# Where two operands of a matmul lie: the x tiles moved in front of the weights, 448 bytes apart modulo 512

## The chip, the cores and the metric

The kernel runs on one core of a Trainium2 chip. The metric is the device time of one execution in microseconds (us), given as the median of several runs. The engines are called PE (matmul), PEld (its weight loads), DVE, ACT, POOL and SP, as the profile calls them. Here SP issues the DMAs.

## What is computed

The reference has two stages. The first is a state space layer over 4 batches of 8 heads, 768 tokens, head width 32 and state width 16. For each chunk of tokens

```
y_intra = (C B^T * exp(cum_i - cum_j) * causal) @ x
y_inter = (C @ state) * exp(cum)
state   = exp(sum(log a)) * state + sum_j(B_j x_j^T * exp(cum_end - cum_j))
```

The second is a feed-forward layer over the resulting 3072 tokens of width 256:

```
h = x @ w_in          # 256 -> 2048
g = h - tanh(h)
out = g @ w_out       # 2048 -> 256
```

All inputs and the output are float32. The weights arrive as float64 bits.

## The kernel before

**State space layer.** A batch is cut into chunks of 112 tokens, 7 to a batch, the last of them 96 wide: 28 chunks. The first 16 rows of a chunk's operand hold the state that the chunk before left, so that one product of a chunk gives y_intra and y_inter at once. In `chunk_a`, PE makes the decay and the C B^T products (`att`, L459 and L465), ACT the exponential, DVE the product, POOL the causal cut, all in `lt`. In `chunk_y`, PE multiplies `lt` with `x` (L502, eight matmuls, one for each head) and then makes the state products, `x` with the weighted B in `bw` (L510, eight small matmuls). ACT copies the state to the next chunk's `x` (`fn_c`, L515), and ACT and DVE split y in two parts (`fn_h`, `fn_l`): `xh`, which holds y rounded to the type of the fast matmul (fp32r), and `xl`, the rest. The last chunk of a batch has no successor, and its state products are left out: `if not last:`.

**Feed-forward layer.** The weights are turned from float64 bits to the same two parts, `wh` and `wl`, which stay in the on-chip memory for the whole run (`conv`). A *step* is one slice of 128 of the 2048 hidden features for a tile of 512 tokens (256 in the first, narrow tiles). `mm1` (L553) is the first product: for each half k of the 256 inputs the matmuls `wh x xh` and `wl x xh`, and then `wh x xl` for both halves, six matmuls of 128 x 128 weights by 512 streamed columns, summed in one result buffer `ph`. ACT and DVE make g from `ph` and split it in `gh` and `gl`. `mm2` (L611) is the second product of a step: `wh x gh`, `wl x gh` and `wh x gl`, each for both halves of the 256 outputs, in the buffers `o` and `oe`: six matmuls again. PE loads the weights of the next matmul (PEld) while the current one streams.

**Order.** The class `Order` records every operation with its engine, a cost in microseconds and what it reads and writes. A list scheduler with random trials under a fixed seed (`plan`) sets the order in which they are issued on every engine. Its costs are constants of the code: the costs of `chunk_y` on PE are 0.5 for the last chunk of a batch and 0.7 for the others.

**Memory.** Tiles are placed one after the other in the order in which they are made. The tiles of the pool `cp` come first, `wh`, `wl`, `xh`, `xl` at its head; those of the other pools, `gh` and `gl` among them, lie behind. The addresses of the built programs, in bytes within a partition, and what is left of them modulo 512:

| tile | bytes | before: at | mod 512 | after: at | mod 512 |
|---|---|---|---|---|---|
| wh | 32768 | 16512 | 128 | 41152 | 192 |
| wl | 32768 | 49280 | 128 | 73920 | 192 |
| xh | 12288 | 82048 | 128 | 16512 | 128 |
| xl | 12288 | 94336 | 128 | 28800 | 128 |
| gh (first of 3) | 2048 | 216256 | 192 | 216704 | 128 |
| gl (first of 3) | 2048 | 222400 | 192 | 222848 | 128 |

A matmul of 512 columns streams 2048 bytes of `xh`, `xl`, `gh` or `gl` from a multiple of 512 behind the tile's start (1024 in the x tiles), and its weights are 512 bytes of `wh` or `wl`, again from a multiple of 512. So the distance of the streamed operand from the weights, modulo 512, is the same for all matmuls of a product: 0 in `mm1` and 64 in `mm2` before.

Of the kernel before, what the change touches and what calls it, by code (L numbers as in the profile page):

```python
# [10 lines left out]
F32 = mybir.dt.float32  # L11
F32R = mybir.dt.float32r
# [8 lines left out]
P = 128  # L21
NB, H, S, D, N = 4, 8, 768, 32, 16
# [7 lines left out]
NCK = NB * CPB  # L30
# [13 lines left out]
NPH, NL, NSW, NRAW, NGB, LAG, WARM = 2, 3, 4, 2, 3, 2, 8  # L44
SWEEPS = 0, 2, 4, 6, 8
NARROW = 1


class Order:
# [12 lines left out]
    def slot(self, tag, bufs):  # L62
        k = self.count[tag] = self.count.get(tag, -1) + 1
        self.fresh[f"{tag}#{k}"] = tag, f"{tag}#{k - bufs}"
        return f"{tag}#{k}"
# [144 lines left out]
def tile_ssm_moe(ctx: ExitStack, tc: tile.TileContext, a, x, bn, bc, wts, out):  # L210
    nc = tc.nc
    cp = ctx.enter_context(tc.tile_pool(name="cp", bufs=1))
# [73 lines left out]
            op("SP", 0.42, lambda i=i: fn(i), w=[name[i]], dma=4 * KB)  # L286


    wh = cp.tile([P, NCONV, 2, 2, 256], F32R, name="wh")
    wl = cp.tile([P, NCONV, 2, 2, 256], F32R, name="wl")  # L290
    xh = cp.tile([P, 2, 2 * S], F32R, name="xh")
    xl = cp.tile([P, 2, 2 * S], F32R, name="xl")

    def conv(u, halves=False):
        raw, n = raws[u, 0], 2 if halves else 1
# [68 lines left out]
    def qlen(ck):  # L364
        return QL if ck % CPB == CPB - 1 else Q
# [119 lines left out]
    def chunk_y(ck):  # L485

        d, k, q = grp[ck // CPG], chs[ck], qlen(ck)
        b, c = divmod(ck, CPB)
        cg = ck % CPG
        n_y = slot("y", 1) if ck in early else slot("ph", NPH)  # L490
        last = c == CPB - 1
        if c == 0:
            seq[b]["n_xh"] = op.pieces(slot("xh", 2), CPB)
            seq[b]["n_xl"] = op.pieces(slot("xl", 2), CPB)
        n_xh, n_xl = seq[b]["n_xh"][c], seq[b]["n_xl"][c]

        def fn():
            pool, tag = (ps_y, "y") if ck in early else (ps_h, "ph")
            y = k["y"] = pool.tile([P, 2 * H * D], F32, tag=tag, name=f"y{ck}")
            for hg in range(2):  # L500
                for h in range(4):
                    nc.tensor.matmul(out=y[D * h : D * h + D, hg * Q : hg * Q + q],  # L502
                                     lhsT=d["x"][:, cg, P * hg + D * h : P * hg + D * h + D],
                                     rhs=k["l"][:, 4 * hg + h, 0:q], start=True, stop=True)
            if not last:

                for w in range(2):
                    for i in range(4):
                        h = 2 * i + w
                        nc.tensor.matmul(out=y[D * i : D * i + N, H * D + D * w : H * D + D * w + D],  # L510
                                         lhsT=d["b"][:, cg, N * h : N * h + N], rhs=d["x"][:, cg, D * h : D * h + D],
                                         start=True, stop=True)

        def fn_c(i):
            nc.scalar.copy(grp[(ck + 1) // CPG]["x"][0:N, (ck + 1) % CPG, 2 * D * i : 2 * D * i + 2 * D],  # L515
                           k["y"][D * i : D * i + N, H * D : H * D + 2 * D])

        at = b % 2 * S + c * Q

        def fn_h():  # L520
            k["yv"] = k["y"][:, 0 : 2 * Q].rearrange("p (g q) -> p g q", g=2)[:, :, 0:q]
            nc.scalar.copy(xh[:, :, at : at + q], k["yv"])

        def fn_l():
            nc.vector.tensor_tensor(out=xl[:, :, at : at + q], in0=k["yv"],  # L525
                                    in1=xh[:, :, at : at + q].bitcast(F32), op=ALU.subtract)

        op("PE", 0.5 if last else 0.7, fn, r=[*k["n_l"], d["p_x"][cg], d["n_bw"]], w=[n_y])
        if not last:
            for i in range(4):  # L530
                op("ACT", 0.2, lambda i=i: fn_c(i), r=[n_y], w=[grp[(ck + 1) // CPG]["p_x"][(ck + 1) % CPG]])
        op("ACT", 0.36, fn_h, r=[n_y], w=[n_xh])
        op("DVE", 0.4, fn_l, r=[n_y, n_xh], w=[n_xl])
# [305 lines left out]
    for s, (i, j) in enumerate(zip(SWEEPS, SWEEPS[1:])):  # L839
        for w in narrow if s < NARROW else wide[: NSW * TT // TW]:  # L840
            segs.append((w, tuple(range(2 * i, 2 * j, TW // w[1]))))
# [84 lines left out]
```

## Time and profile before

| | |
|---|---|
| median of 3 runs | 348.45 us (347.52 to 348.57) |
| the profiled execution | 346.68 us |
| its span, first to last instruction | 345.0 us |
| mean granted TensorE clock | 0.98 |
| matmul records | 2700 (a float32 matmul has two, an fp32r or bf16 one has one) |
| PE busy, DVE busy, ACT busy | 95%, 66%, 56% of the span |

The busy share of PE comes from matmuls whose ends are modelled and which overlap, so it says that PE is not waiting, and not how fast it is. How fast it is shows in the distance of two starts in the timeline. Where the timeline joins two matmuls of one form in a row (x2), the row's start is that of the first.

### The profile page before, as it was taken

The page shows a single profiled execution, that of the slowest core. Times are in us where ns is not written, and L with a number is a line of the kernel's source. Part 1 is how long each engine was busy: PE and PEld are TensorE (multiplying, and loading weights), DVE is VectorE, ACT ScalarE, POOL GpSimd, SP SyncE. Part 2 cuts the span into 40 slices and gives each one's busy share as a digit, 9 for nine tenths or more (in the row PEclk, how much of TensorE's full clock was granted, in tenths as well). Part 3 has the DMA queues.
Part 4 walks back from the last instruction along what each step waited for, and adds up shares of the span by engine and source line. Part 5 has one row for each costly group of instructions (what it writes and reads, how often), then busy time and mean ns, then how long its engine had stood idle before and what let it go on. Part 6 is the DMA issues. An engine that isn't in the chain of part 4 may idle for free.

```text
span 345.0 us, 6725 instructions
## 1 busy us (share of the span) xinstructions
PE 326.9 (95%) x2700; PEld 264.6 (77%) x2700; DVE 229.4 (66%) x335; ACT 194.6 (56%) x399; POOL 55.4 (16%) x69
## 2 busy tenths in 40 slices
PE   7757889899999999999999999999999999999995
PEld 6647779787777878777777777777787777888883
DVE  5899989998889876654545656545655553644461
ACT  8876668786565535444555555545555553534441
POOL 1564534241001030000021111011110101000000
PEclk9978969999999999999999999999999999999999
DMA  6958593614101010111110131100010000010001
GB/s 172 299 163 233 133 260 88 217 34 137 42 0 30 1 46 10 51 63 44 28 36 0 31 91 30 30 2 2 0 63 2 2 0 0 2 61 0 2 0 61
DMA packets 10734, 21.25 MB, mean 62 GB/s; under 512 B 2656, under 2 KB 4384, under 8 KB 10704
## 3 DMA queue, kind: packets, MB, share of 16 engines
q1 hardware_dynamic: 10704, 20.84, 20.9%
q8 instruction: 21, 0.34, 0.4%
q14 instruction: 9, 0.07, 0.1%
HBM read 17.51 MB, written 3.32 MB: 60 GB/s over the span
## 4 chain that ended last, share of the span: by engine, by line
PE 86%; DVE 5%; DMA 4%; ACT 2%; issue 1%; SPq 1%; ACTq 0%
PE ph L553 39%; PE o L611 21%; PE oe L611 18%; PE y L502 4%; PE att L465 3%; DMA x<-x_d 2%; DMA raw<-w_d 2%; PE att L459 1%; DVE lt L473 1%; DVE g L573 1%; ACT x L515 1%; DVE wl L328 1%; PE y L510 1%; DVE rt_c L437 1%; DVE wm L317 1%
## 5 line engine op out<-in xcount | busy, mean ns | idle before, releaser
L569 ACT ACTIVATE g<-ph 128x512 f32<-128x512 f32 x96 | 57.5, 599 | 90.1 <-PE ph L553 82.9
L573 DVE TENSOR_TENSOR g<-ph,g 128x512 f32<-128x512 f32 x96 | 66.0, 690 | 61.0 <-ACT g L569 60.6
L583 DVE TENSOR_TENSOR gl<-g,gh 128x512 fp32r<-128x512 f32 x96 | 68.6, 720 | 27.4 <-ACT gh L577 26.3
L553 PE MATMUL ph<-xh,wh 128*128 128x512 f32 (+1 forms) x208 | 81.8, 395 | 0.4 <-DVE g L573 0.4
L553 PE MATMUL ph<-xh,wl 128*128 128x512 f32 (+1 forms) x208 | 79.5, 384 | 0.6 <-DVE wl L328 0.6
L577 ACT CAST gh<-g 128x512 fp32r<-128x512 f32 x96 | 59.2, 618 | 30.9 <-DVE g L573 25.4
L553 PE MATMUL ph<-xl,wh 128*128 128x512 f32 (+1 forms) x208 | 61.8, 379 | 0.0
L476 POOL TENSOR_SCALAR_AFFINE_SELECT lt<-lt 128x896 f32<-128x896 f32 (+1 forms) x25 | 31.7, 1267 | 163.0 <-DVE lt L473 163.0
L553 PEld LDWEIGHTS ph<-xh,wh 128*128 128x128 f32 x208 | 40.7, 196 | 8.8 <-DVE g L573 0.6
L553 PEld LDWEIGHTS ph<-xh,wl 128*128 128x128 f32 x208 | 40.6, 195 | 7.8 <-DVE wl L328 0.9
L553 PEld LDWEIGHTS ph<-xl,wh 128*128 128x128 f32 x208 | 39.1, 195 | 8.0
L611 PE MATMUL o<-gh,wh 128*128 128x512 f32 (+1 forms) x120 | 42.2, 384 | 0.0
L611 PE MATMUL o<-gh,wl 128*128 128x512 f32 (+1 forms) x120 | 39.6, 363 | 0.0
L611 PE MATMUL o<-gl,wh 128*128 128x512 f32 (+1 forms) x120 | 39.2, 359 | 0.0
L611 PE MATMUL oe<-gh,wh 128*128 128x512 f32 x88 | 34.7, 395 | 0.0
L611 PE MATMUL oe<-gh,wl 128*128 128x512 f32 x88 | 34.6, 394 | 0.0
L611 PE MATMUL oe<-gl,wh 128*128 128x512 f32 x88 | 34.6, 393 | 0.0
L473 DVE TENSOR_TENSOR lt<-att,lt 128x896 f32<-128x896 f32 (+1 forms) x25 | 26.6, 1065 | 4.0 <-ACT lt L469 3.8
L515 ACT COPY x<-y 16x64 f32<-16x64 f32 x96 | 19.5, 204 | 11.0 <-DVE xl L525 6.2
L611 PEld LDWEIGHTS o<-gh,wh 128*128 128x128 f32 x120 | 20.9, 188 | 5.2 <-DVE pt L632 0.4
L611 PEld LDWEIGHTS o<-gh,wl 128*128 128x128 f32 x120 | 20.9, 188 | 4.0
L469 ACT ACTIVATE lt<-att 128x896 f32<-128x896 f32 (+1 forms) x25 | 22.6, 903 | 2.3 <-PE att L465 1.4
(78 smaller groups left out, 326.4 us busy)
## 6 DMA issues: line engine op xcount, KB each, us to landing
raw<-w_d SPq DMA_DIRECT2D x16, 512.0 KB
x<-x_d SPq DMA_DIRECT2D x14, 256.0 KB
bc<-bc_d SPq DMA_DIRECT2D x56, 60.0 KB
out_d<-ob SPq DMA_DIRECT2D x12, 256.0 KB
braw<-bn_d SPq DMA_DIRECT2D x14, 112.0 KB
cum<-parts SPq DMA_DIRECT2D x1, 168.0 KB
lt_c<-cum SPq DMA_DIRECT2D x4, 27.0 KB
rt_c<-cum SPq DMA_DIRECT2D x4, 27.0 KB
```

The lines of the kernel that those rows point to most:

```text
L465: nc.tensor.matmul(out=at_[:, i, 2 + w, :], lhsT=bb[r, w], rhs=cc[r, w, 0:q], start=True, stop=True)
L469: nc.scalar.activation(k["l"][:, :, 0:q].rearrange("p (i w) q -> p i w q", i=4), k["a"][:, :, 0:2, :], AF.Exp)
L473: nc.vector.tensor_tensor(out=lt, in0=k["a"][:, :, 2:4, :], in1=lt, op=ALU.mult)
L476: nc.gpsimd.affine_select(out=k["l"][:, :, 0:q], in_=k["l"][:, :, 0:q], pattern=[[0, H], [1, q]], compare_op=ALU.is_ge, fill=0.0, base=N, ...
L502: nc.tensor.matmul(out=y[D * h : D * h + D, hg * Q : hg * Q + q], lhsT=d["x"][:, cg, P * hg + D * h : P * hg + D * h + D], rhs=k["l"][:, 4 ...
L515: nc.scalar.copy(grp[(ck + 1) // CPG]["x"][0:N, (ck + 1) % CPG, 2 * D * i : 2 * D * i + 2 * D], k["y"][D * i : D * i + N, H * D : H * D + ...
L553: nc.tensor.matmul(out=ph[:, j - f % 2, :], lhsT=w_[:, u, 0, k, j * P : (j + 1) * P], rhs=(xh, xl)[p][:, k, ts], start=p == 0 and k == 0 a ...
L569: nc.scalar.activation(g, gs[w, f][0], AF.Tanh)
L573: nc.vector.tensor_tensor(out=g, in0=ph, in1=g, op=ALU.subtract)
L577: nc.scalar.copy(gh, gs[w, f][1])
L583: nc.vector.tensor_tensor(out=gl, in0=g, in1=gh.bitcast(F32), op=ALU.subtract)
L611: nc.tensor.matmul(out=po[w, seg][e], lhsT=w_[:, u, 1, j, e * P : (e + 1) * P], rhs=g[:, j - f % 2, :], start=f == seg[0] and k == 0 and j ...
```

## The change

The change has two parts. The tiles `xh` and `xl` are made ahead of `wh` and `wl`. An unused tile of 64 bytes (`AHEAD` is 16 words) lies between them and the weights, and another of 384 bytes behind the weights. With that the distance of the streamed operand from the weights is 448 modulo 512 in both products (table above), and all tiles behind the weights stand 448 bytes higher. The other part: the last of the 28 chunks makes its state products too. They are written to a part of its result buffer that nobody reads. The costs that the scheduler sees stay as they were.

```
+AHEAD = 16
...
+    xh = cp.tile([P, 2, 2 * S], F32R, name="xh")
+    xl = cp.tile([P, 2, 2 * S], F32R, name="xl")
+    cp.tile([P, AHEAD], F32, name="ahead")
     wh = cp.tile([P, NCONV, 2, 2, 256], F32R, name="wh")
     wl = cp.tile([P, NCONV, 2, 2, 256], F32R, name="wl")
-    xh = cp.tile([P, 2, 2 * S], F32R, name="xh")
-    xl = cp.tile([P, 2, 2 * S], F32R, name="xl")
+    cp.tile([P, P - 2 * AHEAD], F32, name="behind")
...
-            if not last:
+            if not last or ck == NCK - 1:
```

The order of the instructions is the same on all engines but for one row on PE. This is the place on PE where the last chunk is multiplied (`y`, from `lt` and `x`), between a second product (`o`, `oe`) and a first (`ph`), before:

```order
1156 L611 MATMUL oe_0_2923<-gl_12_3219,wh 128x512
1157 L502 MATMUL y_3249<-lt_3217,x_2564 32x96 x8
1158 L553 MATMUL ph_14_3258<-xh,wh 128x512
1159 L553 MATMUL ph_14_3258<-xh,wl 128x512
1160 L553 MATMUL ph_14_3258<-xh,wh 128x512
```

And after the change:

```order
1156 L614 MATMUL oe_0_2925<-gl_12_3221,wh 128x512
1157 L505 MATMUL y_3251<-lt_3219,x_2566 32x96 x8
1158 L513 MATMUL y_3251<-x_2566,bw_2568 16x32 x8
1159 L556 MATMUL ph_14_3268<-xh,wh 128x512
1160 L556 MATMUL ph_14_3268<-xh,wl 128x512
```

Eight matmuls of 16 x 32 results stand between the chunk's product and the next step; line numbers are three higher.

## The prediction

> **What bounds the kernel now.** I read the page's totals first, then its chain of waits, then the table of stretches.
>
> ```profile
> span 345.0 us, 6725 instructions
> PE 326.9 (95%) x2700; PEld 264.6 (77%) x2700; DVE 229.4 (66%) x335; ACT 194.6 (56%) x399; POOL 55.4 (16%) x69
> PEclk9978969999999999999999999999999999999999
> PE 86%; DVE 5%; DMA 4%; ACT 2%; issue 1%; SPq 1%; ACTq 0%
> ...
> 62.00:340.70 278.70, 277.50 (x1969) 220.11 (x1967) 174.56 (x250) 146.95 (x288) 29.31 (x31) 1.00 0.10 31
> ...
> 290.95:339.10 48.15, 48.15 (x210) 39.17 (x209) 25.15 (x37) 22.11 (x37) 0.00 (x0) 1.00 0.03 12
> ```
>
> The columns of the last two rows are the stretch, its length, the busy time and count of PE, PEld, DVE, ACT and POOL, then the granted clock and the DMA load. From 62 us to the end PE lacks work for 1.2 us of 278.7, at a granted clock of 1.00. DVE and ACT have a third and more of the time to spare. So the end is set by how fast PE gets through its matmuls, and what happens in the first 62 us (DMA, the attention of the first tile) is left alone by this change. The groups by shape say how many matmuls there are.
>
> ```profile
> L553 PE MATMUL ph<-xh,wh 128*128 128x512 f32 x176 | 71.1, 404 | 0.4 <-DVE g L573 0.4
> ...
> L611 PE MATMUL oe<-gh,wh 128*128 128x512 f32 x88 | 34.7, 395 | 0.0
> ...
> L553 PE MATMUL ph<-xh,wh 128*128 128x256 f32 x32 | 10.7, 347 | 0.0
> ```
>
> A 512-wide step of the first product has six matmuls, two of them of this form: 88 steps. One of the second product has one of this form among its six: 88 steps. That is 176 steps and 1056 matmuls. The durations of 395 to 404 ns are no help, because matmuls overlap and their ends are modelled. What counts is from start to start, and that is read from the timeline (start, length, instruction).
>
> ```profile
> 290.73 0.40 PE L611 MATMUL o<-gh,wh 128*128 128x512 f32 x1
> ...
> 339.20 0.39 PE L611 MATMUL o<-gh,wh 128*128 128x512 f32 x1
> ```
>
> Between these two starts lie the 210 matmuls of the last row of the table above and nothing else: 48.47 us / 210 = 230.8 ns each, 1.385 us for a step. Over the 1056 this pace is 243.7 us of the 345.0, so one nanosecond of pace is worth 1.06 us of the total.
>
> The pace is not the same everywhere. Here are starts of steps, and four starts inside steps.
>
> ```profile
> 72.15 0.39 PE L553 MATMUL ph<-xh,wh 128*128 128x512 f32 x1
> ...
> 73.51 0.28 PE L611 MATMUL o<-gh,wh 128*128 128x256 f32 x1
> ...
> 199.78 0.40 PE L611 MATMUL o<-gh,wh 128*128 128x512 f32 x1
> ...
> 201.17 0.39 PE L611 MATMUL o<-gh,wh 128*128 128x512 f32 x1
> 201.40 0.39 PE L611 MATMUL oe<-gh,wh 128*128 128x512 f32 x1
> 201.62 0.39 PE L611 MATMUL o<-gh,wl 128*128 128x512 f32 x1
> ...
> 202.54 0.40 PE L553 MATMUL ph<-xh,wh 128*128 128x512 f32 x1
> ...
> 203.00 0.40 PE L553 MATMUL ph<-xh,wh 128*128 128x512 f32 x1
> 203.24 0.40 PE L553 MATMUL ph<-xh,wl 128*128 128x512 f32 x1
> ...
> 203.93 0.40 PE L553 MATMUL ph<-xh,wh 128*128 128x512 f32 x1
> ...
> 205.31 0.40 PE L611 MATMUL o<-gh,wh 128*128 128x512 f32 x1
> ...
> 335.08 0.39 PE L611 MATMUL o<-gh,wh 128*128 128x512 f32 x1
> ```
>
> A step whose predecessor was of the other product takes 1.39 us (199.78 to 201.17, a second product behind a first; 202.54 to 203.93, the reverse). A first product behind another first takes 1.38 (203.93 to 205.31). The first product at 72.15, which ends a run of first products, takes 1.36 (to 73.51), or 226.7 ns a matmul. A second product behind another second takes 1.37, and the three from 335.08 to 339.20 take 4.12 us, or 228.9 ns a matmul. Single distances go from 0.22 us (201.40 to 201.62) to 0.24 (203.00 to 203.24). So the same instruction with the same operand sizes is slowest just after a change of product and settles when the product stays. What changes with the product, among other things, is the distance of the streamed operand from the weights: 0 bytes modulo 512 in the first product, 64 in the second.
>
> **The change part by part.** *The layout* puts this distance at 448 in both products. It adds no instruction and no transfer. If the slow step after a change of product comes from the jump between distances 0 and 64, the jump is gone and all steps run at a settled pace. No row has a pair at distance 448, so its settled pace is bounded. The nearest rows are the two settled ones: 226.7 ns at distance 0 (448 is 64 bytes from it) and 228.9 at distance 64 (the same 64 bytes, on the other side). I take the middle, 228 ns: 230.8 - 228 = 2.8 ns, times 1056 = -3.0 us. The outer bounds are the single distances. If all went at about 225 (the 0.22 rows), it would be 1056 x 5.8 = -6.1 us. If all went at 236 (the 0.24 rows), 1056 x 5.2 = +5.5 us. The 192 matmuls of 256 columns (32 of the form above, of 12 in a step) get the same distance, and I leave them at nothing: a nanosecond on each is 0.2 us.
>
> All tiles behind the weights move up by 448 bytes, and with them the operands of DVE and ACT. I take nothing for it: in the stretch from 290.95 DVE is busy 25.15 of 48.15 us, and an engine that became a tenth slower would still fit. Without that cover, a tenth on DVE would be 2.5 us there.
>
> *The last chunk's state products* are eight small matmuls on PE, with no DMA and no new wait: the state weights they read were loaded for the chunk before as well. Their price is read from two places where PE goes from one step through a chunk to the next.
>
> ```profile
> 274.31 0.40 PE L611 MATMUL oe<-gl,wh 128*128 128x512 f32 x1
> 274.64 0.59 PE L502 MATMUL y<-lt,x 128*32 128x112 f32 x16
> 275.05 0.30 PE L510 MATMUL y<-x,bw 128*16 128x32 f32 x16
> 275.27 0.50 PE L553 MATMUL ph<-xh,wh 128*128 128x512 f32 x1
> ...
> 288.44 0.40 PE L611 MATMUL oe<-gl,wh 128*128 128x512 f32 x1
> 288.77 0.54 PE L502 MATMUL y<-lt,x 128*32 128x96 f32 x16
> 289.24 0.50 PE L553 MATMUL ph<-xh,wh 128*128 128x512 f32 x1
> ...
> 289.73 0.36 DVE L525 TENSOR_TENSOR xl<-y,xh 128x192 fp32r<-128x192 f32 x1 [0.86 <-ACT xh L522]
> ```
>
> With the products it is 275.27 - 274.31 = 0.96 us, without them (the very chunk that gets them) 289.24 - 288.44 = 0.80. Part of the 0.16 is that chunk's greater width (112 against 96), so I take +0.13. PE has no idle time there, so it counts in full. Behind it, on ACT and DVE, wait the copies of this chunk to xh and xl. They end at 290.09 now, and at about 290.22 then. The next matmuls are steps of the tile before, several microseconds of them, so nobody waits for this.
>
> The sum against the profiled execution: 346.68 us (span 345.0 and 1.7 around it) - 3.0 + 0.13 = 343.8. The median of the runs shown is 348.45, which lies 1.8 above the profiled one. The same difference of 2.87 there gives **345.6**.
>
> **The rivals.** *The distance does not count.* For it: a change of product also changes the streamed tiles, the weights' order and the result buffers (one ph, or o and oe in turn), any of which may set the phase of the pace; and over 210 matmuls the two products, at different distances, cannot be told apart by more than a few ns a step. Against it: steps with the same tiles differ by what ran before them. Then only the +0.13 is left: 348.6. The Trainium skill has a rule for this rival (TensorE: Matmul & The Clock Gate, "Step-by-step: what each phase is for"): TensorE reads the streamed operand and the weights through two independent ports, and loading the next weights takes no read bandwidth from the running matmul. By that rule the sum is the 348.6. The trace neither confirms nor refutes it, since no row here has the same step at two layouts.
>
> *448 is on the wrong side.* At 0 and at 64 the stream starts level with, or ahead of, the weights that are loaded beside it. At 448 it starts 64 bytes behind their place. If the two reads get in each other's way, a stream that must overtake the load in every matmul loses each time. The slow distances then become the rule: 234 ns, halfway between the slowest step (1.39 us, 231.7) and the 0.24 rows (236), gives 1056 x 3.2 = +3.4, with the products 352.0. It decides from a pace of 231.7 ns on, where +0.9 us and the products reach 1 us. For it: no pair in this trace has the stream behind the weights. Against it: the pace differs by just 2 ns between the two distances that are there.
>
> That the layout isn't what the words say is ruled out by the addresses of the built program; and the order on every engine is the old one but for the eight products.
>
> **How the numbers follow.** Settled pace, 345.6: 0.48. No effect, 348.6: 0.28. Wrong side, 352.0: 0.24. The 0.3% that a measurement of this kernel can tell is 1.05 us. The settled pace stays within it if it comes out above 229.9 ns, and the wrong side below 231.7: I give 0.02 and 0.01 of theirs to no change. That is faster 0.46, same 0.31, slower 0.23. For the range, the likeliest case alone goes from 342.5 (nearly the -6.1) to 347.4. The whole range has to take in no effect and the larger part of the wrong side: 342.5 to 351.5, which leaves about 0.1 above and 0.07 below.
>
> **What would show it.** Right: a step takes 1.36 to 1.375 us whatever ran before it, and the 210 matmuls of the last stretch take less than 48.1 us. If 1.39 stays for steps behind the other product, the jump was not the cause. If steps take over 1.39 us, the stream pays for each overtaking. The way through the last chunk should read about 0.93 instead of 0.80. The granted clock should stay at 1.00; another clock would make all of this void.

## The result: slower by 0.7%

| | before | after |
|---|---|---|
| median, 12 runs each | 347.98 us | 350.01 us |
| ratio, 95% interval | | 1.0071 (1.0042 to 1.0099) |
| span of the profiled execution | 345.0 us | 347.8 us |
| mean granted clock | 0.980 | 0.973 |
| from start to start, last 210 matmuls | 230.8 ns | 233.3 ns |

The forecast was 345.6 us, faster than before. The time lies within the range that was given, but the kernel became slower. The runs of one kernel spread by about 1% with the clock that was granted, but the clock is not what makes the difference: nine runs of the kernel before at a mean of 0.970 or 0.971, taken beside the experiments, lie from 348.18 to 348.89 us, and the changed kernel's four at 0.971 from 350.52 to 351.35. These are the totals of the page after the change, and two rows of its table of stretches (the stretch, its length, busy time and count of PE, PEld, DVE, ACT and POOL, clock, DMA):

```profile
span 347.8 us, 6757 instructions
PE 330.7 (95%) x2716; PEld 265.6 (76%) x2716; DVE 230.0 (66%) x335; ACT 194.4 (56%) x399; POOL 55.8 (16%) x69
PEclk9958989899999999999999999999999999999999
PE 86%; DVE 5%; DMA 4%; ACT 1%; issue 1%; SPq 1%; ACTq 0%
...
293.25:341.95 48.70, 48.70 (x210) 39.03 (x209) 25.14 (x37) 22.11 (x37) 0.00 (x0) 1.00 0.03 11
62.00:343.00 281.00, 279.67 (x1973) 219.87 (x1972) 174.00 (x249) 145.73 (x285) 28.32 (x31) 0.99 0.10 29
```

The shares are nearly the same as before, and PE again lacks work for little more than 1 us (1.33) between 62 us and the end. In the last stretch DVE and ACT do the same work in the same time (25.14 against 25.15 us, 22.11 against 22.11). So nothing new is waited for. PE itself is slower, which the busy shares do not show. Starts of steps do, in the timeline after the change:

```profile
293.05 0.39 PE L614 MATMUL o<-gh,wh 128*128 128x512 f32 x1
...
302.85 0.39 PE L556 MATMUL ph<-xh,wh 128*128 128x512 f32 x1
...
304.25 0.39 PE L556 MATMUL ph<-xh,wh 128*128 128x512 f32 x1
...
305.64 0.39 PE L614 MATMUL o<-gh,wh 128*128 128x512 f32 x1
...
307.05 0.39 PE L614 MATMUL o<-gh,wh 128*128 128x512 f32 x1
...
308.44 0.39 PE L614 MATMUL o<-gh,wh 128*128 128x512 f32 x1
...
342.05 0.39 PE L614 MATMUL o<-gh,wh 128*128 128x512 f32 x1
```

The step at 302.85 is a first product behind a second, 304.25 a first behind a first, 305.64 a second behind a first, 307.05 a second behind a second. All four take 1.39 to 1.41 us. What ran before a step no longer matters, as forecast. But the one pace that is left is (342.05 - 293.05) / 210 = 233.3 ns, 1.400 us a step, and before it was 230.8. Over 1056 matmuls 2.5 ns would be 2.65 us.

What the whole run lost is read from a longer stretch, with the same two matmuls as its ends in both traces: the first matmul of the second 512-wide step, and the start with which the last 210 end. The columns are the stretch, its length, the busy time and count of PE, the granted clock, the DMA share and GB/s. Before, and after the change:

```profile
70.66:339.20 268.54, 268.54 (x1856) 1.00 0.09 26
```

```profile
70.98:342.05 271.07, 271.07 (x1873) 1.00 0.09 26
```

At the same clock of 1.00, and with PE busy throughout, it became 2.53 us longer. The state products are 0.12 of it (below), so the layout costs 2.4 us over these 1044 matmuls, 2.3 ns for each. The spans differ by 2.8 us because the changed execution was already 0.32 us late at the start of this stretch; ahead of it the clock was not 1.00 throughout in either execution.

### The profile page after: what moved, and what is told of

Same layout as the page of the kernel before. It is cut to its first block, busy times and chain, and to the rows that moved or that the text cites. A ratio compares the mean times of both kernels' runs of the same rounds, so it can differ in the third digit from the quotient of the medians.

```text
span 347.8 us, 6757 instructions
## 1 busy us (share of the span) xinstructions
PE 330.7 (95%) x2716; PEld 265.6 (76%) x2716; DVE 230.0 (66%) x335; ACT 194.4 (56%) x399; POOL 55.8 (16%) x69
## 4 chain that ended last, share of the span: by engine, by line
PE 86%; DVE 5%; DMA 4%; ACT 1%; issue 1%; SPq 1%; ACTq 0%
PE ph L556 39%; PE o L614 21%; PE oe L614 18%; PE y L505 4%; PE att L468 3%; DMA x<-x_d 3%; DMA raw<-w_d 1%; PE att L462 1%; DVE lt L476 1%; DVE g L576 1%; DVE wl L331 1%; PE y L513 1%; DVE rt_c L440 1%; ACT x L518 1%; DVE wm L320 1%
## 5 line engine op out<-in xcount | busy, mean ns | idle before, releaser
L556 PE MATMUL ph<-xl,wh 128*128 128x512 f32 (+1 forms) x208 | 63.3, 386 | 0.0
L479 POOL TENSOR_SCALAR_AFFINE_SELECT lt<-lt 128x896 f32<-128x896 f32 (+1 forms) x25 | 30.7, 1228 | 163.5 <-DVE lt L476 163.5
L614 PEld LDWEIGHTS o<-gl,wh 128*128 128x128 f32 x120 | 21.0, 190 | 4.0
```

Source lines behind the costliest of these rows:

```text
L479: nc.gpsimd.affine_select(out=k["l"][:, :, 0:q], in_=k["l"][:, :, 0:q], pattern=[[0, H], [1, q]], compare_op=ALU.is_ge, fill=0.0, base=N, ...
L556: nc.tensor.matmul(out=ph[:, j - f % 2, :], lhsT=w_[:, u, 0, k, j * P : (j + 1) * P], rhs=(xh, xl)[p][:, k, ts], start=p == 0 and k == 0 a ...
L614: nc.tensor.matmul(out=po[w, seg][e], lhsT=w_[:, u, 1, j, e * P : (e + 1) * P], rhs=g[:, j - f % 2, :], start=f == seg[0] and k == 0 and j ...
```

## The experiments

All kernels differ from the changed one or the one before in the unused tiles that set the distances, and in nothing else unless it is said. "Pace" is (end - start) / 210 over the same 210 matmuls: from the first second product after the step that follows the last chunk, to the start of the same instruction 35 steps on. The medians carry the spread with the granted clock, so the pace is read from the traces, where the clock in that stretch was 1.00 in every run. In the edits shown, the sizes of the unused tiles stand as numbers, where the code of the runs has constants.

Two theories stood at first. *Distance*: each distance has a settled pace of its own, and 448 happens to have a bad one. *One distance for all*: it is the equality of the distances that locks PE at 233.3 ns.

**Both at 0.** In the changed kernel

```
-    cp.tile([P, AHEAD], F32, name="ahead")
...
-    cp.tile([P, P - 2 * AHEAD], F32, name="behind")
+    cp.tile([P, 112], F32, name="behind")
```

> The changed kernel with both products at distance 0 (no tile between x and weights, 448 bytes behind the weights). Theory 'distance': a uniform distance has a pace of its own, and the run of first products before the change showed 226.7 ns a matmul at 0; then steps take 1.36 us and the time is 347.98 - 1056 x 4.1 ns + 0.13, about 343.8 us. Theory 'one distance for all': any single distance locks the steps at the 1.400 us (233.3 ns) that 448 showed, so about 350.0 us.

Measured: 343.7 us, ratio to before 0.9896 (0.9853 to 0.9938). Its timeline:

```profile
288.01 0.39 PE L613 MATMUL o<-gh,wh 128*128 128x512 f32 x1
...
335.62 0.39 PE L613 MATMUL o<-gh,wh 128*128 128x512 f32 x1
```

47.6 us for 210 matmuls: 226.7 ns, 1.360 us a step. The distance theory gave 343.8. That the median meets it to 0.1 us is chance, since the six runs lie from 341.91 to 345.37. The long stretch, 268.54 us before, is

```profile
70.51:335.62 265.11, 265.09 (x1873) 1.00 0.09 27
```

That is 3.43 us shorter with the state products in it, where 4.1 ns on each of its 1044 matmuls would be 4.3 us less. So the kernel before is, over the whole run, less slow than its last 210 matmuls.

**Both at 64.** 448 bytes ahead of the weights and none behind:

```
-    cp.tile([P, AHEAD], F32, name="ahead")
+    cp.tile([P, 112], F32, name="ahead")
...
-    cp.tile([P, P - 2 * AHEAD], F32, name="behind")
```

> The changed kernel with both products at distance 64 (448 bytes between x and the weights, nothing behind them). Theory 'distance': the pace of second products behind second products before the change, 228.9 ns, steps of 1.373 us, about 347.98 - 1056 x 1.9 ns + 0.13 = 346.1 us. Theory 'one distance for all': 1.400 us and 350.0 us as at 448.

Measured: 346.02 us, ratio 0.9975 (0.9946 to 1.0003), so not told apart from before by its time. The pace is 228.9 ns, just what second products behind second products had before the change:

```profile
290.51 0.39 PE L613 MATMUL o<-gh,wh 128*128 128x512 f32 x1
...
338.58 0.39 PE L613 MATMUL o<-gh,wh 128*128 128x512 f32 x1
```

**Both at 256.** The two unused tiles are 64 and 48 words.

> The changed kernel with both products at distance 256, as far from level as it can be modulo 512. Theory 'distance', with a stream that is slowed where it meets the weight load: fewest or latest meetings, a pace at or under 228.9 ns, 346 us or less. Theory 'one distance for all': 1.400 us a step, 350.0 us.

Measured: 344.39 us, ratio 0.9903 (0.9868 to 0.9938), pace 226.7 ns:

```profile
288.24 0.39 PE L614 MATMUL o<-gh,wh 128*128 128x512 f32 x1
...
335.84 0.39 PE L614 MATMUL o<-gh,wh 128*128 128x512 f32 x1
```

Three more kernels with one distance for all matmuls have paces of 226.7, 228.9 and 226.7 ns, none of them 233.3: the theory of one distance for all falls.

**The layout without the products.** The changed kernel with the old condition:

```
-            if not last or ck == NCK - 1:
+            if not last:
```

> The changed kernel without the state products of the last chunk, so the layout alone. If the layout makes the loss, steps stay at 1.400 us and the time is 0.13 us under the changed kernel's, about 349.9 us. If the products change the pace of what follows them, the steps behind the last chunk differ from 1.400 us (52 us of the run; at 1.385 a gain of 0.5 us).

Measured: 350.03 us, ratio 1.0083 (1.0049 to 1.0116), against 350.01 with the products. The pace is 233.3 ns again:

```profile
294.59 0.39 PE L614 MATMUL o<-gh,wh 128*128 128x512 f32 x1
...
343.58 0.39 PE L614 MATMUL o<-gh,wh 128*128 128x512 f32 x1
```

So the layout alone makes the loss. What the products cost is too little for the medians. The long stretch shows it, with 271.07 us in the changed kernel and without the products

```profile
72.64:343.58 270.94, 270.94 (x1856) 1.00 0.08 26
```

and so does the way through the last chunk in the changed kernel:

```profile
290.63 0.40 PE L614 MATMUL oe<-gl,wh 128*128 128x512 f32 x1
290.96 0.54 PE L505 MATMUL y<-lt,x 128*32 128x96 f32 x16
291.31 0.30 PE L513 MATMUL y<-x,bw 128*16 128x32 f32 x16
291.54 0.50 PE L556 MATMUL ph<-xh,wh 128*128 128x512 f32 x1
```

0.91 us, where it was 0.80 before. The two readings give 0.13 and 0.11, about 0.12 us.

**What shape has the curve?** The rival of the prediction, a stream that has to overtake the weight load, would have the pace worst a little behind the weights' place and good ahead of it. Three distances try it: 480 (32 bytes behind; tiles of 8 and 104 words), 384 (128 behind; 32 and 80 words), and 32 ahead (the x tiles behind the weights, 8 words between, 112 behind).

> Both products at distance 480: the stream starts 32 bytes behind the weights' place. So far the steps were 1.360 us at 0 and 256, 1.373 at 64, 1.400 at 448. Theory 'overtaking' (a stream that starts a little behind the weight load is slowed until it is past it): 1.38 us or more, between 448 and 0 or above both. Theory 'place in a small period' (what counts is the distance modulo 128, so that 0 and 256 are free, and 64 and 448 are not): 480 is a new place modulo 128 (96) and can be anything, but 384 must then be free.

> Both products at distance 384: the stream starts 128 bytes behind the weights' place. Theory 'overtaking': still in the weights' way, 1.38 to 1.42 us a step, a time like the changed kernel's 350. Theory 'place in a small period' (modulo 128): free, 1.360 us a step, a time like the 343.7 at distance 0.

> Both products at distance 32, the x tiles behind the weights as in the kernel before (32 bytes between them, 448 behind the x tiles). Theory 'overtaking': the stream starts ahead, so between the steps at 0 and 64, 1.360 to 1.373 us. Theory 'nearness' (bad close to level on both sides, level itself excepted): over 1.373 us.

Measured, one run each, so the pace is what counts: 349.38, 348.65 and 349.48 us. In this order their timelines:

```profile
292.92 0.40 PE L614 MATMUL o<-gh,wh 128*128 128x512 f32 x1
...
341.92 0.40 PE L614 MATMUL o<-gh,wh 128*128 128x512 f32 x1
```

```profile
292.39 0.39 PE L614 MATMUL o<-gh,wh 128*128 128x512 f32 x1
...
341.19 0.39 PE L614 MATMUL o<-gh,wh 128*128 128x512 f32 x1
```

```profile
293.02 0.39 PE L614 MATMUL o<-gh,wh 128*128 128x512 f32 x1
...
342.02 0.39 PE L614 MATMUL o<-gh,wh 128*128 128x512 f32 x1
```

233.3 ns at 480, 232.4 at 384, 233.3 at 32. The paces at 480 and 384 are as overtaking had them, and the one at 32 is not: a stream 32 bytes ahead is as slow as one 64 behind, so overtaking falls. A period of 128 falls too, since 384 is not free. A period of 256 was left, with nearness not yet excluded.

**A jump between two good distances.** First products at 0, second products at 256 (no tile ahead, 48 words behind).

> First products at distance 0, second products at 256, which both gave 1.360 us a step when used alone. If the jump from one distance to another costs by itself, steps behind a change of product take 1.37 to 1.39 us, as before the change. If it is the distances' own pace that counts, and a jump only shows between distances of unequal pace, all steps take 1.360 us.

Measured: 343.16 us in one run, pace 226.7 ns, every step of the stretch at 1.360 us:

```profile
288.10 0.39 PE L613 MATMUL o<-gh,wh 128*128 128x512 f32 x1
...
335.70 0.39 PE L613 MATMUL o<-gh,wh 128*128 128x512 f32 x1
```

The jump itself costs nothing. The slow steps before the change came from going between 0 and 64, two places that are not the same modulo 256.

**A period of 256?** 320 should then be what 64 is, and 128 what 384 is (tiles of 48 and 64 words, and of 96 and 16).

> Both products at distance 320. So far, us a step: 0 1.360, 32 1.400, 64 1.373, 256 1.360, 384 about 1.396, 448 1.400, 480 1.400. Theory 'overtaking' fell with 32 and 256. Theory 'period 256' (what counts is the distance modulo 256): 320 is 64 there, so 1.373 us a step and a time near that at 64, 346. Theory 'only whole multiples of 256 are free, the rest is chance': anything from 1.37 to 1.41.

> Both products at distance 128. Theory 'period 256': 128 is what 384 is there, so uneven steps of 1.385 to 1.398 us. Otherwise another pace, 1.360 if the period were 128 with 384 spoilt by something else.

Measured, one run each: 346.92 and 350.26 us. At 320, and then at 128:

```profile
291.39 0.39 PE L614 MATMUL o<-gh,wh 128*128 128x512 f32 x1
...
339.46 0.39 PE L614 MATMUL o<-gh,wh 128*128 128x512 f32 x1
```

```profile
293.97 0.39 PE L614 MATMUL o<-gh,wh 128*128 128x512 f32 x1
...
342.77 0.39 PE L614 MATMUL o<-gh,wh 128*128 128x512 f32 x1
```

228.9 ns, the pace at 64, and 232.4, the pace at 384. Three pairs that are equal modulo 256 (0 and 256, 64 and 320, 128 and 384) have equal paces, so a period of 256 bytes holds for the pairs that were tried. Nearness falls, since the pace at 128 is slower than at 64.

**Which weights count?** The weights of a matmul are loaded (PEld) beside the matmul in front of it: in the trace before, those for the matmul at 339.20 from 338.97 to 339.16. So a stream could meet the load of the next weights, or the place of its own could count. To tell them apart `wl` was moved 64 bytes up, so that the streams are at 0 from `wh` and at 448 from `wl` (the kernel with both at 0, with 16 words between the weight tiles and 96 behind).

> As with both at distance 0, but wl stands 64 bytes higher, so that the streams are at 0 from wh and at 448 from wl. This tells which weights count. If it is the weights loaded beside the stream, those of the next matmul: slow (over 0.230 us to the next start) are the matmuls in front of one with wl: in the first product the 1st and 3rd of six, in the second product the 2nd and 3rd. If it is the matmul's own weights: the 2nd and 4th, and the 3rd and 4th. Total between the two uniform cases, steps of 1.37 to 1.39 us.

Measured: 348.11 us in one run, pace 231.7 ns or 1.390 us a step, between the two uniform cases as expected. But the order of slow and quick matmuls fits neither. Here is a second product (from its `wh` matmul at 307.30) and the start of the first product behind it:

```profile
307.30 0.39 PE L614 MATMUL o<-gh,wh 128*128 128x512 f32 x1
307.53 0.39 PE L614 MATMUL oe<-gh,wh 128*128 128x512 f32 x1
307.76 0.40 PE L614 MATMUL o<-gh,wl 128*128 128x512 f32 x1
308.00 0.39 PE L614 MATMUL oe<-gh,wl 128*128 128x512 f32 x1
308.23 0.39 PE L614 MATMUL o<-gl,wh 128*128 128x512 f32 x1
308.46 0.39 PE L614 MATMUL oe<-gl,wh 128*128 128x512 f32 x1
308.69 0.40 PE L556 MATMUL ph<-xh,wh 128*128 128x512 f32 x1
308.92 0.39 PE L556 MATMUL ph<-xh,wl 128*128 128x512 f32 x1
309.15 0.40 PE L556 MATMUL ph<-xh,wh 128*128 128x512 f32 x1
309.39 0.40 PE L556 MATMUL ph<-xh,wl 128*128 128x512 f32 x1
309.62 0.62 PE L556 MATMUL ph<-xl,wh 128*128 128x512 f32 x2
```

In the second product the third takes longest (0.24 us, the others 0.23). That place is slow by both readings. In the first product the third takes 0.24 here. Over the 29 first products of this trace that stand behind a second one with nothing in between, the third and the fourth are longest (234 and 235 ns on average, the others 229 to 233), one expected by each reading. Single distances say little in any case: at 64 for all they go from 225 to 232 ns. This stays open.

**The good distance alone.** The kernel before with one unused tile:

```
     xl = cp.tile([P, 2, 2 * S], F32R, name="xl")
+    cp.tile([P, 112], F32, name="behind")
```

> The kernel before with one unused tile of 448 bytes behind the x tiles and nothing else: x stays behind the weights, no added products, and both products come to distance 0. If the distance alone counts, and not that x moved in front: steps of 1.360 us, the time at distance 0 with x in front less 0.1 for the products, 343.6 us, and faster than before and changed kernel.

Measured: 344.96 us (341.84 to 345.63), ratio 0.9919 (0.9887 to 0.9951). The 343.6 that was expected lies within the spread of the runs, and the median 1.4 us above it. The pace is 226.8 ns:

```profile
288.50 0.39 PE L612 MATMUL o<-gh,wh 128*128 128x512 f32 x1
...
336.12 0.39 PE L612 MATMUL o<-gh,wh 128*128 128x512 f32 x1
```

It beats the kernel before and the changed one. Its interval overlaps that of the kernel with x in front and both at 0, so where the x tiles stand makes no difference that was seen.

All paces together, by the distance of both products from the weights:

| distance | 0 | 32 | 64 | 128 | 256 | 320 | 384 | 448 | 480 |
|---|---|---|---|---|---|---|---|---|---|
| modulo 256 | 0 | 32 | 64 | 128 | 0 | 64 | 128 | 192 | 224 |
| ns a matmul | 226.7 | 233.3 | 228.9 | 232.4 | 226.7 | 228.9 | 232.4 | 233.3 | 233.3 |

The place of either tile alone does not give these paces. With the weights at 128 modulo 512, streams at 128, at 160, at 192 (second products of the kernel before, behind one another) and at 384 (second products of the kernel with 0 and 256) have 226.7, 233.3, 228.9 and 226.7 ns. With the streams at 128 the pace changes with the place of the weights. And the distance of 64 has 228.9 ns with streams and weights at 192 and 128 as well as at 128 and 64.

**The narrow matmuls.** The traces also hold matmuls of 256 columns, 12 to a step. Here are such a second product and the start of the step behind it, with both at 0, and then in the changed kernel:

```profile
73.39 0.64 PE L613 MATMUL o<-gh,wh 128*128 128x256 f32 x4
...
74.82 0.40 PE L555 MATMUL ph<-xh,wh 128*128 128x512 f32 x1
```

```profile
73.89 0.62 PE L614 MATMUL o<-gh,wh 128*128 128x256 f32 x4
...
75.26 0.39 PE L556 MATMUL ph<-xh,wh 128*128 128x512 f32 x1
```

That is 1.43 us at 0 and 1.37 at 448, 119 and 114 ns a matmul, at a clock of 1.00. So the order of good and bad distances is not the same at this width: here 448 is the quicker one.

## Why the prediction was wrong

- *What bounds the kernel, and what one nanosecond of pace is worth* (1.06 us): right. The reference of 230.8 ns was a little too slow for the whole run, since it is read from the last 210 matmuls alone: both at 0 gained 3.43 us in the long stretch, with the state products in it, and not the 4.2 that 230.8 gives. The paces at 0 and at 64, put in the same sum, gave 343.8 and 346.1 us against medians of 343.7 and 346.02, which is closer than the spread of the runs can show.
- *The slow steps behind a change of product come from the jump of distance*: right that they go when the distance is one for all. The reason is narrower than it was put. A jump from 0 to 256 costs nothing; from 0 to 64 it does.
- *The settled pace at 448*: this is the step that failed. "I take the middle, 228 ns" came from the two nearest rows, and nearness in bytes is no guide. 448 is 192 modulo 256, a place at which the kernel before has no matmul at all. Its pace is 233.3 ns, inside the outer bounds of 225 and 236 and above everything the two rows span. The term was -3.0 us. It measures +2.4 in the long stretch, and would be +2.65 at the difference of the last 210 matmuls.
- *The matmuls of 256 columns*: left at nothing. They did change, and became quicker: 114 ns in the step shown, where the same step before takes 1.42 us (73.51 to 74.93), 118 ns. All but 12 of the 192 lie ahead of the long stretch, where PE also waits for other things, and what they gave there is not known.
- *The state products*: +0.13 forecast, about 0.12 in the traces.
- *DVE, ACT and the tiles moved by 448 bytes*: nothing forecast, and nothing seen.
- *The rival "448 is on the wrong side"* has the right sign and nearly the right pace (234 ns, 352.0 us), with a mechanism that fell: 32 bytes ahead of the weights is as slow as 64 behind. So its nearness is luck. By the prediction's own sign (steps over 1.39 us mean that the stream overtakes) the 1.400 us would have been read as proof of it.
- *The rival "the distance does not count"* fell. The changed kernel and the one with both at 0 issue the same instructions in the same order, and differ by 6.6 ns in each matmul and by 6 us in the time. The rule of the Trainium skill that stood beside it (TensorE: Matmul & The Clock Gate, "Step-by-step: what each phase is for") would have the two alike, so the time does not come out by it. The runs don't show which two accesses meet, so whether the load disturbs the stream, which the rule denies, stays open.
- *The pace from which the settled case counts as no change*: 229.9 ns was given, and 229.7 comes out, since the +0.13 of the products went in with the wrong sign. Only 0.02 of a chance rested on it.

The chances were 0.46 for faster and 0.23 for slower. With bounds on both sides and no row at the new place, 0.46 was more than the rows could carry.

## What to carry to other kernels

Where PE sets the end, read from start to start and not the busy time: 230.8 and 233.3 ns a matmul both read as 95% busy. For fp32r matmuls of 128 x 128 weights and 512 columns that each load their own weights, put the streamed tiles and the weight tiles a multiple of 256 bytes apart; a single unused tile did that here and gave 0.8%. It is no rule for other shapes: with 256 columns 448 was quicker than 0, and other types were not tried. A row at one address says nothing of another nearby (226.7 ns at 0, 233.3 at 32), so measure the place itself before rearranging a memory.

## What was not expected of the hardware

The time from one 128x512 matmul of this type to the next depends on the distance of streamed operand and weights modulo 256 bytes: 226.7 ns at 0, 228.9 at 64, 232.4 at 128, 233.3 at 32, 192 and 224. With equal distances a step with nothing in between repeats to a nanosecond or so; at 128 and 384 steps go from 1.385 to 1.400 us, and their mean repeats. Where the products are at 0 and 64, the pace takes some matmuls to settle: a first product behind another first still takes 1.38 us, where 1.360 is the settled step. At 256 columns the distances rank otherwise (119 ns at 0, 114 at 448). What meets what inside the chip, the streamed operand with the weights that are loaded or with something else, stays open.
